# Linear attention ahead of a gated convolution: channels on partitions, four heads on quarters of the array, norms by way of DRAM

## The chip, the cores and the metric

The kernel runs on one core of a Trainium2 chip. The metric is the device time of one execution in microseconds (us), taken as the median of several runs. A profile is one execution recorded by the hardware profiler; its span reaches from the first to the last instruction. TensorE is called PE (its weight loads PEld), VectorE DVE, ScalarE ACT, GpSimd POOL, SyncE SP.

## What is computed

Three blocks follow one another on 8 batches of 576 tokens. The first is linear attention with 8 heads of 64 channels and a root-mean-square norm on each head; the second is a causal convolution gate over 512 channels; the third mixes along the tokens.

```
kv  = einsum('bhsd,bhse->bhde', k, v)
out = einsum('bhsd,bhde->bhse', q, kv)
x   = out / sqrt(mean(out * out, -1) + 1e-6) * g_norm      # heads side by side: 512 channels
gate = sigmoid(sum_k conv_w[k] * x shifted by 4-k tokens)
x   = (gate * (x @ w_val)) @ w_out
theta = x @ w_theta
y   = w_tok_r @ (x * cos(theta)) + w_tok_i @ (x * sin(theta))
u   = x + y;  result = u + max(u @ w_ch, 0)
```

The arrays come in float32, the weights in float64 words that the kernel decodes to float32 itself. Large products are made in three passes of float32r (high times high, low times high, high times low); the attention's own products are float32, which the trace shows as two records per product.

## The kernel before

The work has two stages. Stage one goes over the batches i = 0 to 7 and makes, for each, attention, value product, gate and output product; its result goes to DRAM (ydram). Stage two reads it back and does the token mixing (theta, u, c). The change lies in stage one alone.

In stage one the four weight chunks of w_val (wv) and of w_out (wo) are fetched, decoded on DVE (L92 to L96) and split into high and low parts (L67, L68). In one pass of the loop (L346) these steps follow one another on PE:

- attention(i+1), L173: for each of five chunks of 128 tokens (the last has 64) four products q times bd, where bd holds the kv of two heads on the diagonal of a 128x128 block. The result o has tokens on partitions and 512 channels along the row. ACT or DVE takes the squares and sums them per head (L184, L185, L189), twelve small DVE instructions make 1/sqrt by an integer start and three Newton steps (L197 to L203), and DVE multiplies o by it into xn (L207).
- value(i), L246: twelve products for each of four blocks m of 128 output channels and each half h of 288 tokens (v, L242 to L244), gated on DVE (g, L255) and split (gh, gl). The gate of block m comes from conv (L229): one ACT instruction, four DVE instructions (acc, L233), a sigmoid on ACT. Two convs are made ahead, the other two within value.
- key_value, L157: k times v for pairs of heads of later batches (kvp, L166), on two halves of the array's columns, three or four pairs in a pass.
- transposes(i+1), L214: xn is transposed on PE (xt, L222), which brings channels onto partitions; ACT writes xh and x, DVE the low part xl (L226). Then come two convs.
- first(i), L261: the output product (y), moved by ACT (yo, L267) and stored by SP.

PSUM is one pool of eight banks, given out in turn. A scheduler places each engine's instructions; waits on one engine's list are in order, and SP issues nearly all transfers in one list. The decoding of the weights of stage two (tk, wt) is put in at low priority in passes 1 to 5.

Of the kernel before, what the change touches and what calls it, by code (L numbers as in the profile page):

```python
# [11 lines left out]
I32 = mybir.dt.int32  # L12
# [12 lines left out]
CH = [(c * P, min(P, S - c * P)) for c in range(5)]  # L25
# [17 lines left out]
SUMS_ON_VECTOR = (range(5), (2, 4), ())  # L43
# [5 lines left out]
def attention_moe_holo_kernel(ctx, tc, kvm, kvt, qt, gn, w_val, conv_w, w_out, w_th, w_tok, w_ch, outT):  # L49
# [20 lines left out]
    def fetch(pool, src, width, name, tag=""):  # L70
# [31 lines left out]
    def weight_chunk(pool, tiles, src, k, name, scale=None, raw=None):  # L102
# [4 lines left out]
        if scale is None:  # L107
# [5 lines left out]
    ident = con.tile([P, P], F32, tag="ident", name="ident")  # L113
    make_identity(nc, ident)
# [11 lines left out]
    stdram = [dr.tile([P, DM], F32, tag=f"st{b}", name=f"st{b}") for b in range(0, B, 2)]  # L126
    tokdram = dr.tile([P, 9 * S], F32, tag="td", name="td")
# [5 lines left out]
    bds = []  # L133
    for i in range(NBD):
        t = pa.tile([P, NP, P], F32, tag=f"bd{i}", name=f"bd{i}")
        nc.gpsimd.memset(t, 0.0)
        bds.append(t)
# [19 lines left out]
    def key_value(b, kv, p0=0):  # L157

        ps = bank(f"kvp{b}_{p0}")
# [8 lines left out]
        bd = bds[b % NBD]  # L168
        psv = ps[:, 0:n * D].rearrange("p (a e) -> p a e", a=n)
        nc.scalar.activation(bd[0:D, p0:p0 + n, 0:D], psv[0:D], AF.Copy)  # L170
        nc.scalar.activation(bd[D:P, p0:p0 + n, D:P], psv[D:P], AF.Copy)

    def attention(b, q):  # L173
        bd = bds[b % NBD]
        ss = px.tile([P, 5, 8], F32, tag="ss", bufs=2, name=f"ss{b}")
        nc.gpsimd.memset(ss[D:P, 4, :], 1.0)
        po = []
        for c, (s0, n) in enumerate(CH):
            o = bank(f"o{b}_{c}")
            for p in range(NP):  # L180
                nc.tensor.matmul(o[:n, p * P:(p + 1) * P], q[p][:, s0:s0 + n], bd[:, p, :], start=True, stop=True)  # L181
# [382 lines left out]
```

## Time and profile before

| what | value |
|---|---|
| three runs | 754.7 to 756.11 us, median 755.47 us |
| the profiled execution's own time | 757.18 us |
| its span | 755.4 us |
| PE busy | 726.1 us (96%) |
| DVE busy | 534.8 us (71%) |
| ACT busy | 391.7 us (52%) |
| DMA | 97.58 MB, mean 129 GB/s |

Busy time is the union of an engine's records, and records of PE overlap, since a product's end is modelled; so the steps from start to start are what PE really spends. A busy time divided by its count is the cost of one instruction in a dense run; the mean is the length of one record. Idle time of an engine is put down to what ended last ahead of it.

### The profile page before, as it was taken

To read this page: it belongs to the slowest core of one execution; us is meant where nothing else is said; L and a number is where in the kernel's file an instruction comes from. 1 tells how busy PE (TensorE), PEld (TensorE's weight loads), DVE (VectorE), ACT (ScalarE), POOL (GpSimd) and SP (SyncE) were. 2 spreads that over 40 slices of the span, in tenths; PEclk is the share of its full clock that TensorE was granted. 3 is DMA by queue.
4 is the path that set the end of the run, shared out by engine and by line. 5 is a ranking of instruction groups with operands and counts; after the bars stand their busy time and mean duration, and the time that the engine had idled before them with its cause. 6 is when DMAs were issued, how large, how long until landed. Compare 5 with 4: busy or idle time off the path is not lost.

```text
span 755.4 us, 14634 instructions
## 1 busy us (share of the span) xinstructions
PE 726.1 (96%) x5584; PEld 697.9 (92%) x5584; DVE 534.8 (71%) x1045; ACT 391.7 (52%) x1173; POOL 16.4 (2%) x64
## 2 busy tenths in 40 slices
PE   2798999999999999999999999999999999999998
PEld 1797899999999999979899899899999999998998
DVE  4698888989899989769883873853853934936504
ACT  2366779787787876466541650621732513614301
POOL 2001000000000000000000000000000000000000
PEclk9889999999999999999999999999999999999999
DMA  9868644655544126634327034063051161160101
GB/s 297 274 190 271 215 160 139 203 186 170 178 139 149 64 89 161 209 109 120 127 88 205 2 125 112 19 187 87 17 162 61 62 169 50 58 177 4 64 1 63
DMA packets 77542, 97.58 MB, mean 129 GB/s; under 512 B 11168, under 2 KB 50208, under 8 KB 77472
## 3 DMA queue, kind: packets, MB, share of 16 engines
q1 hardware_dynamic: 76896, 94.55, 40.9%
q0 software_dynamic: 576, 2.10, 0.9%
q8 instruction: 44, 0.72, 0.4%
q14 instruction: 26, 0.21, 0.1%
HBM read 65.66 MB, written 30.97 MB: 128 GB/s over the span
## 4 chain that ended last, share of the span: by engine, by line
PE 88%; DMA 4%; ACT 4%; DVE 3%; issue 0%; SPq 0%; POOL 0%; DVEq 0%; ACTq 0%; POOLq 0%
PE u L467 10%; PE u L466 10%; PE u L465 10%; PE c L244 4%; PE c L242 4%; PE c L243 4%; PE v L242 4%; PE y L242 4%; PE o L181 4%; PE v L243 4%; PE y L243 4%; PE v L244 4%; PE y L244 4%; PE th L413 3%; PE th L411 3%; PE th L412 3%
## 5 line engine op out<-in xcount | busy, mean ns | idle before, releaser
L470 DVE TENSOR_TENSOR f<-u,f 128x288 f32<-128x288 f32 x64 | 26.5, 454 | 131.8 <-PE u L467 131.7
L67 ACT ACTIVATE uh<-f 128x288 fp32r<-128x288 f32 x64 | 26.1, 443 | 155.7 <-DVE f L470 155.7
L233 DVE SCALAR_TENSOR_TENSOR acc<-x,cw,acc 128x576 f32<-128x576 f32 x128 | 95.6, 810 | 1.1 <-ACT acc L231 1.1
L242 PE MATMUL y<-gh,woh 128*128 128x288 f32 x256 | 76.9, 302 | 1.6 <-ACT woh L67 0.9
L242 PE MATMUL v<-xh,wvh 128*128 128x288 f32 x256 | 77.4, 302 | 0.0
L243 PE MATMUL v<-xh,wvl 128*128 128x288 f32 x256 | 76.4, 298 | 0.0
L243 PE MATMUL y<-gh,wol 128*128 128x288 f32 x256 | 76.3, 299 | 0.0
L244 PE MATMUL v<-xl,wvh 128*128 128x288 f32 x256 | 75.8, 296 | 0.0
L244 PE MATMUL y<-gl,woh 128*128 128x288 f32 x256 | 75.6, 297 | 0.0
L242 PE MATMUL c<-uh,wch 128*128 128x288 f32 x256 | 75.4, 295 | 0.0
L244 PE MATMUL c<-ul,wch 128*128 128x288 f32 x256 | 75.4, 295 | 0.0
L243 PE MATMUL c<-uh,wcl 128*128 128x288 f32 x256 | 75.4, 294 | 0.0
L189 ACT ACTIVATE junk<-o 128x64 f32<-128x64 f32 (+1 forms) x264 | 55.1, 250 | 4.2 <-PE o L181 3.5
L189 ACT ACTIVATION_READ_ACCUMULATOR junk<-o 128x1 f32 (+1 forms) x264 | 53.7, 232 | 0.0
L242 PEld LDWEIGHTS y<-gh,woh 128*128 128x128 f32 x256 | 48.5, 190 | 2.5 <-ACT woh L67 1.0
L413 PE MATMUL th<-wth,yl 128*128 128x512 f32 x128 | 50.2, 393 | 0.0
L411 PE MATMUL th<-wth,yh 128*128 128x512 f32 x128 | 50.1, 391 | 0.0
L412 PE MATMUL th<-wtl,yh 128*128 128x512 f32 x128 | 50.0, 391 | 0.0
L242 PEld LDWEIGHTS v<-xh,wvh 128*128 128x128 f32 x256 | 48.9, 191 | 1.2 <-ACT junk L189 1.0
L243 PEld LDWEIGHTS v<-xh,wvl 128*128 128x128 f32 x256 | 48.9, 191 | 0.0
L243 PEld LDWEIGHTS y<-gh,wol 128*128 128x128 f32 x256 | 48.8, 191 | 0.1
L244 PEld LDWEIGHTS v<-xl,wvh 128*128 128x128 f32 x256 | 48.8, 191 | 0.0
(189 smaller groups left out, 2115.2 us busy)
## 6 DMA issues: line engine op xcount, KB each, us to landing
kv<-in_kvm_dram SPq DMA_DIRECT2D x32, 512.0 KB, 6.5
q<-in_qt_dram SPq DMA_DIRECT2D x32, 288.0 KB, 4.8
yd<-yo SPq DMA_DIRECT2D x64, 144.0 KB, 2.3
f<-yd SPq DMA_DIRECT2D x32, 288.0 KB, 3.4
out_dram<-f SPq DMA_DIRECT2D x64, 144.0 KB, 1.8
sd<-fT SPq DMA_DIRECT2D x64, 128.0 KB, 2.5
yt<-sd SPq DMA_DIRECT2D x8, 1024.0 KB, 5.4
raw_tk<-in_w_tok_dram SPq DMA_DIRECT2D x10, 512.0 KB, 5.4
```

Of the source, the lines that this page charges most:

```text
L181: nc.tensor.matmul(o[:n, p * P:(p + 1) * P], q[p][:, s0:s0 + n], bd[:, p, :], start=True, stop=True)
L189: nc.scalar.activation(junk[:n], o[:n, h * D:(h + 1) * D], AF.Square, scale=0.125, accum_out=ss[:n, c, h:h + 1])
L233: nc.vector.scalar_tensor_tensor(a, x[:, m, k:k + S], cw[:, m * 5 + k:m * 5 + k + 1], a, ALU.mult, ALU.add)
L242: nc.tensor.matmul(ps[:, :HS], wh[:, m, ks], xh[:, k, tsl], start=(k == 0), stop=False)
L243: nc.tensor.matmul(ps[:, :HS], wl[:, m, ks], xh[:, k, tsl], start=False, stop=False)
L244: nc.tensor.matmul(ps[:, :HS], wh[:, m, ks], xl[:, k, tsl], start=False, stop=(k == 3))
L411: nc.tensor.matmul(ps, yh[:, k, :], wth[0][:, k, :], start=(k == 0), stop=False)
L412: nc.tensor.matmul(ps, yh[:, k, :], wth[1][:, k, :], start=False, stop=False)
L413: nc.tensor.matmul(ps, yl[:, k, :], wth[0][:, k, :], start=False, stop=(k == 3))
L465: nc.tensor.matmul(ps[:, :HS], zh[:, ms], wkh[:, j, sl], start=(i == 0), stop=False)
L466: nc.tensor.matmul(ps[:, :HS], zh[:, ms], wkl[:, j, sl], start=False, stop=False)
L467: nc.tensor.matmul(ps[:, :HS], zl[:, ms], wkh[:, j, sl], start=False, stop=(i == 8))
```

## The change

- q times kv is turned round: kv of a head pair (kvs, 64x64 each) is the stationary operand and q moves in halves of 288 tokens, so that o has channels on partitions. Four heads use the four quarters of the array: the rows by the head's place in its pair, the columns by the pair (tile_position). A block o_h_g takes a pair of PSUM banks, for half h of the tokens and half g of the channels.
- The transposes (xt) and the identity are gone. ACT writes squares (sq) and, times g_norm, x itself from o.
- The sums of squares are made on PE: 64 products per batch with an indicator (ind) of 32 columns, each over 36 tokens, on quarters of the array's columns (ss, L219).
- The twelve DVE instructions stay, on 128x36. Their result y goes to DRAM (rd) and comes back spread over the 64 channels of each head (yb, 1.18 MB in two transfers). DVE then multiplies x by yb (L247), ACT and DVE split it (xh, xl).
- Channels now lie in another order: head pairs are mixed in blocks of 128. So the rows and columns of wv, wo and the conv weights are fetched in that order (mixed=True), in four transfers per chunk, half issued by SP and half by ACT.
- PSUM of stage one is three pairs of banks (o, v, y in turn) and two single banks (kvp, sums). v, g, gh, gl, yo are made for 576 tokens at once instead of twice 288. The kv buffers go from five to four.
- attention(i+1) is a generator: value(i) runs one block of it ahead of each m.

The names in the rows below carry the buffer number at the end; o_0_1 is half 0, channel half 1. On PE, in pass 2, this is where y of batch 2 ends and v begins, after the change:

```order
L266 MATMUL y_3_1940<-gl_1553,woh 128x288
L206 MATMUL o_0_0_2030<-q_0_1532,kvs_1359 64x288 x2
L206 MATMUL o_0_0_2030<-q_1_1534,kvs_1359 64x288 x2
L264 MATMUL v_0_2038<-xh_1834,wvh 128x288
L265 MATMUL v_0_2038<-xh_1834,wvl 128x288
L206 MATMUL o_0_1_2073<-q_2_1536,kvs_1359 64x288
L266 MATMUL v_0_2038<-xl_1835,wvh 128x288
```

Before, the twenty products of o stood in one run between y and v; now they lie in pieces between the products of v, two of which stand ahead of the first that needs xl.

On DVE, ahead of the last batch, before the change (y_3663 is 1/sqrt, acc the conv, fT belongs to stage two; the g and gl are the last of batch 6):

```order
L207 TENSOR_TENSOR xn_4_3686<-o_4_3649,y_3663 64x512
L68 TENSOR_TENSOR gl_3689<-g_2_3770,gh_3688 128x288
L255 TENSOR_TENSOR g_3_3803<-v_3_0_3804,acc_3_3763 128x288
L255 TENSOR_TENSOR g_3_3803<-v_3_1_3820,acc_3_3763 128x288
L226 TENSOR_TENSOR xl_3839<-x_3836,xh_3838 128x4x128
L68 TENSOR_TENSOR gl_3689<-g_3_3803,gh_3688 128x288 x2
L226 TENSOR_TENSOR xl_3839<-x_3836,xh_3838 128x4x128 x3
L226 TENSOR_TENSOR xl_3839<-x_3836,xh_3838 128x4x64
L275 STREAM_TRANSPOSE fT_0_4031<-f_4026 128x1024
L233 SCALAR_TENSOR_TENSOR acc_0_3880<-x_3836,cw,acc_0_3880 128x576
```

and after it:

```order
L69 TENSOR_TENSOR gl_3376<-acc_3_3459,gh_3375 128x576
L231 TENSOR_TENSOR t_3576<-t_3576,hm_3577 128x36
L232 SCALAR_TENSOR_TENSOR y_3575<-t_3576,y_3575 128x36
L247 TENSOR_TENSOR x_3377<-x_3377,yb_3591 128x2x576 x2
L69 TENSOR_TENSOR xl_3623<-x_3377,xh_3622 128x1152
L255 SCALAR_TENSOR_TENSOR acc_0_3630<-x_3377,cw,acc_0_3630 128x576
L69 TENSOR_TENSOR xl_3623<-x_3377,xh_3622 128x1152
```

The multiplication by 1/sqrt (xn before, x<-x,yb now) stood ahead of the last g and gl of batch 6; now it comes behind them, and the trip by DRAM lies between 1/sqrt and it, with no other instruction for DVE in between.

On SP, the trip itself in pass 5, after the change:

```order
L234 DMA rd_96<-y_3151 128x36
L421 DMA td<-dst_tk_2462 128x512
L291 DMA yd_75<-yo_0_3288 128x576
L93 DMA raw_tk_2925<-in_w_tok_dram 128x1024
L238 DMA yb_3167<-rd_96 64x4x576 x2
L291 DMA yd_75<-yo_1_3316 128x576
```

None of rd and yb was there before; yb stands behind the first store of y and a weight load.

The core of the diff:

```diff
+    ind = pa.tile([P, 16, 32], F32, tag="ind", name="ind")
+    nc.gpsimd.memset(ind, 0.0)
+    for i in range(2):
+        for t in range(16):
+            nc.gpsimd.memset(ind[i * D:(i + 1) * D, t, 16 * i + t:16 * i + t + 1], 1.0)
...
-            t = px.tile([P, 2, 5, P], F32, tag="kv", bufs=5, name=f"kv{b}_{p}")
+            t = px.tile([P, 2, 5, P], F32, tag="kv", bufs=4, name=f"kv{b}_{p}")
...
+        for h in range(2):
+            sl = slice(h * HS, (h + 1) * HS)
+            for g in range(2):
+                o = two_banks(f"o{b}_{h}_{g}")
+                for i in range(2):
+                    for j in range(2):
+                        rows = slice(j * D, (j + 1) * D)
+                        mm = nc.tensor.matmul(o[i * D:(i + 1) * D, j, :], kv[rows, 2 * g + i, :], q[2 * g + i][rows, sl],
+                                              start=True, stop=True, tile_position=(j * D, i * D))
+                ch = slice(2 * g, 2 * g + 2)
+                sq[h, g] = px.tile([P, 2, HS], F32, tag="sq", bufs=4, name=f"sq{b}_{h}_{g}")
+                nc.scalar.activation(sq[h, g], o, AF.Square, scale=0.125)
+                nc.scalar.activation(x[:, ch, PAD + h * HS:PAD + (h + 1) * HS], o, AF.Copy, scale=gsb)
+                if (h, g) != (1, 1):
+                    yield x
+
+        with tc.issue_after(mm.ins):
+            for t in range(16):
+                for k in range(NM):
+                    ts = slice(t % 8 * TB, (t % 8 + 1) * TB)
+                    nc.tensor.matmul(sums[32 * k:32 * (k + 1), :], ind[:, t, :], sq[t // 8, k // 2][:, k % 2, ts],
+                                     start=(t == 0), stop=(t == 15), tile_position=(0, 32 * k))
...
+        nc.sync.dma_start(out=rdram[b], in_=y)
+        yb = px.tile([P, NM, S], F32, tag="yb", bufs=1, name=f"yb{b}")
+        for i in range(2):
+            src = rdram[b].rearrange("(k i s) x -> i k (s x)", i=2, s=16)[i]
+            nc.sync.dma_start(out=yb[i * D:(i + 1) * D], in_=src.unsqueeze(0).to_broadcast([D, NM, S]))
+        yield x, yb
+
+    def normalize(b, x, yb):
...
+        for g in range(2):
+            ch = slice(2 * g, 2 * g + 2)
+            v = x[:, ch, PAD:]
+            last = nc.vector.tensor_tensor(v, v, yb[:, ch, :], ALU.mult)
+            parts(xh[:, ch, :], xl[:, ch, :], v)
+        return (x, xh, xl), last
...
         for m in range(NM):
+            between()
+            g = sg[m]
+            ps = two_banks(f"v{b}_{m}")
             for h in range(2):
+                product(ps[:, h], wv, m, xh, xl, h * HS)
+            halves = lambda t: t.rearrange("p (h s) -> p h s", h=2)
+            nc.vector.tensor_tensor(halves(g), ps, halves(g), ALU.mult)
+            parts(gh[:, m, :], gl[:, m, :], g)
```

More of the change, by code (lines that the diff above doesn't have):

```diff
@@ L24 @@
 PAD = 4
-CH = [(c * P, min(P, S - c * P)) for c in range(5)]
+TB = 36
 EPS = 1e-6
@@ L126, in attention_moe_holo_kernel @@
     stdram = [dr.tile([P, DM], F32, tag=f"st{b}", name=f"st{b}") for b in range(0, B, 2)]
+    rdram = [dr.tile([P, TB], F32, tag=f"rd{b}", name=f"rd{b}") for b in range(B)]
     tokdram = dr.tile([P, 9 * S], F32, tag="td", name="td")
@@ L157, in key_value @@
     def key_value(b, kv, p0=0):
-        ps = bank(f"kvp{b}_{p0}")
+        ps = pk.tile([P, 512], F32, tag="pk", name=f"kvp{b}_{p0}")
         n = len(kv)
@@ L167, in key_value @@
                                      start=(c == 0), stop=(c == 4), tile_position=(0, j * D))
[L168 to L171, printed above, removed]
+        if b not in kvs_of:
+            kvs_of[b] = pa.tile([P, NP, D], F32, tag="kvs", bufs=NBD, name=f"kvs{b}")
+        nc.scalar.activation(kvs_of[b][:, p0:p0 + n, :], ps[:, 0:n * D].rearrange("p (a e) -> p a e", a=n), AF.Copy)
@@ new lines, in attention @@
+        x = pa.tile([P, NM, PAD + S], F32, tag="x", bufs=2, name=f"x{b}")
+        nc.gpsimd.memset(x[:, :, 0:PAD], 0.0)
+        sums = pk.tile([P, 512], F32, tag="pk", name=f"ss{b}")[:, :TB]
+        sq = {}
+        for h in range(2):
[3 more added lines that the diff above has]
+                for i in range(2):
+                    for j in range(2):
+                        rows = slice(j * D, (j + 1) * D)
[7 more added lines that the diff above has]
+                    yield x
@@ L200, in attention @@
+        t = px.tile([P, TB], F32, tag="t", bufs=2, name=f"t{b}")
+        hm = px.tile([P, TB], F32, tag="hm", bufs=2, name=f"hm{b}")
+        nc.vector.tensor_scalar(ss, sums, EPS, None, ALU.add)
+        nc.vector.tensor_scalar(y.bitcast(I32), ss.bitcast(I32), -0.5, RSQRT_BITS, ALU.mult, ALU.add)
+        nc.vector.tensor_scalar(hm, ss, -0.5, None, ALU.mult)
         for _ in range(3):
@@ L365, in attention_moe_holo_kernel @@
             kvs[b, p] = load_kv(b, (p,))[0]
-        if i + 1 < B:
-            xn, last = attention(i + 1, qs.pop(i + 1))
-        if i > 0:
-            gs = value(i, *xs, sg)
+        nxt = attention(i + 1, qs.pop(i + 1)) if i + 1 < B else iter(())
+        if i == 0:
+            gs = value(i, *xs, sg, lambda: None)
+            for k in range(WOFIRST):
+                weight_chunk(px, wo, w_out, k, "wo", raw=raw[f"o{k}"])
+            xyb = list(nxt)[-1]
+        else:
+            got = []
+            gs = value(i, *xs, sg, lambda: got.append(next(nxt, None)))
+            xyb = got[-1]
         if i == 0:
```

136 lines of the change are left out of this document (46 added, 90 removed).

## The prediction

> **What bounds the kernel now.** I read the page's busy times first, then the windows of stage one batch by batch (cut where o of the next batch begins), then PE's timeline, and last DVE's groups and its timeline ahead of the last batch.
>
> ```profile
> span 755.4 us, 14634 instructions
> PE 726.1 (96%) x5584; PEld 697.9 (92%) x5584; DVE 534.8 (71%) x1045; ACT 391.7 (52%) x1173; POOL 16.4 (2%) x64
> ```
>
> ```profile
> core 0: us, PE busy (x) PEld busy (x) DVE busy (x) ACT busy (x) POOL busy (x), PEclk, DMA share, GB/s
> 122.35:156.99 34.64, 34.64 (x314) 33.88 (x313) 32.34 (x68) 28.43 (x124) 1.14 (x5) 1.00 0.57 182
> 156.99:191.94 34.95, 34.93 (x314) 33.85 (x313) 32.09 (x68) 28.32 (x122) 1.14 (x5) 1.00 0.55 179
> 262.12:294.73 32.61, 32.61 (x255) 32.08 (x253) 28.35 (x60) 27.03 (x120) 0.12 (x1) 1.00 0.36 108
> 294.73:320.20 25.47, 25.47 (x195) 25.47 (x193) 21.48 (x41) 9.69 (x23) 1.20 (x2) 1.00 0.69 202
> ```
>
> PE never pauses from 122 to 320 us: five batches take (294.73 - 122.35) / 5 = 34.5 us each. But DVE is busy 32 of these 34.6 us. So stage one is PE's, with DVE 7% behind: a batch in which DVE has to stand and wait for a few us becomes DVE's. The head of the program is another matter:
>
> ```profile
> 0.00:20.00 20.00, 5.07 (x80) 4.51 (x80) 9.30 (x15) 5.42 (x8) 5.42 (x23) 1.00 0.92 301
> 20.00:30.00 10.00, 8.82 (x106) 8.38 (x102) 4.14 (x13) 3.96 (x8) 0.61 (x2) 1.00 0.90 267
> 30.00:40.00 10.00, 7.05 (x46) 6.49 (x47) 9.28 (x24) 4.95 (x10) 0.99 (x4) 0.61 0.58 212
> 60.00:87.00 27.00, 22.85 (x257) 20.84 (x252) 22.75 (x50) 18.66 (x52) 2.65 (x10) 0.94 0.79 247
> ```
>
> There DMA is 0.8 to 0.9 busy and PE idles. Stage two, from 320 us on, is untouched; I give it no change.
>
> **The change part by part.**
>
> *PE's work in a batch.* Rows of PE's timeline:
>
> ```profile
> 86.94 4.75 PE L181 MATMUL o<-bd,q 128*128 128x128 f32 x40
> 104.60 1.97 PE L166 MATMUL kvp<-kv 128*64 128x64 f32 x60
> 106.67 2.90 PE L222 MATMUL xt<-ident,xn 128*128 128x128 f32 x20
> 139.62 0.29 PE L243 MATMUL v<-xh,wvl 128*128 128x288 f32 x1
> 139.75 0.29 PE L244 MATMUL v<-xl,wvh 128*128 128x288 f32 x1
> 279.65 2.30 PE L222 MATMUL xt<-ident,xn 128*128 128x128 f32 x20
> ```
>
> ```profile
> 139.97 0.39 PE L166 MATMUL kvp<-kv 128*64 128x64 f32 x6
> ```
>
> Gone: o 4.7 and xt 2.3 to 2.9, together 7.3 us. Added: 16 products q by kvs, two records each. A record of 128 columns steps by (4.75 - 0.27) / 39 = 0.115 us, 0.9 ns a column, so one of 288 columns costs some 0.25 us. How far do quarters run together? The nearest row is kvp, whose halves alternate two records by two: 60 records of 64 columns step by (1.97 - 0.22) / 59 = 0.030 us, where 0.9 ns a column would be 0.057. So two run at a time. That can be because the array holds just two tiles in that row, or because products start in order and a second record waits for the first of its tile, which then holds back those behind it. I take the second for four quarters: a run of n products costs (n + 1) x 0.25. Three whole blocks (1.25 each) and o_0_1, which the order cuts into 1, 1 and 2 (1.75), make 5.5 us. Each change of tile shape costs 0.22 - 0.13 = 0.09 us (last v at 139.75, kvp at 139.97, against a step of 0.13); six pieces among v are twelve changes, 1.1 us. The 64 sums have two records of 36 columns: between 0.033 (two at a time at 0.9 ns a column) and kvp's 0.060 us a product, I take 0.045, 2.9 us. New: 9.5 us, net +2.2. PE's own period goes from 34.5 to 36.7 us.
>
> The bounds of the quarters: all four at a time, 0.5 us a block (3.0 us with the split block) and sums at 1.1, PE's period is 34.5 - 7.3 + 3.0 + 1.1 + 1.1 = 32.4; one at a time, 16 x 0.5 = 8.0 and 3.8, it is 40.1. The Trainium skill (TensorE: Matmul & The Clock Gate, Part 3: Packing small matmuls) says that products on different row and column groups start some 4 ns apart and all run concurrently; by that rule the 16 products would cost about 2 us. It is weighed as a rival below; kvp's row shows two together and cannot show four.
>
> *The chain by DRAM.* Groups of DVE and transfers that price it:
>
> ```profile
> L233 DVE SCALAR_TENSOR_TENSOR acc<-x,cw,acc 128x576 f32<-128x576 f32 x128 | 95.6, 810 | 1.1 <-ACT acc L231 1.1
> L255 DVE TENSOR_TENSOR g<-v,acc 128x288 f32<-128x288 f32 x64 | 28.6, 451 | 7.1 <-PE v L244 5.3 <-ACT acc L234 1.1 <-ACT junk L189 0.7
> L226 DVE TENSOR_TENSOR xl<-x,xh 128x512 fp32r<-128x512 f32 x32 | 21.8, 682 | 3.2 <-ACT x L225 2.8
> L202 DVE TENSOR_TENSOR t<-t,hm 128x40 f32<-128x40 f32 x24 | 4.8, 198 | 0.2
> L189 ACT ACTIVATE junk<-o 128x64 f32<-128x64 f32 x216 | 45.4, 257 | 4.2 <-PE o L181 3.5
> ```
>
> ```profile
> kv<-in_kvm_dram SPq DMA_DIRECT2D x32, 512.0 KB, 6.5
> yd<-yo SPq DMA_DIRECT2D x64, 144.0 KB, 2.3
> yt<-sd SPq DMA_DIRECT2D x8, 1024.0 KB, 5.4
> td<-dst_tk SPq DMA_DIRECT2D x1, 32.0 KB, 1.4
> ```
>
> From 0.45 at 288 and 0.68 at 512 elements a step of 576 is 0.75 and one of 1152 some 1.34 us. Count from T = 0, the end of the sums. v_3 takes 24 x 0.134 = 3.2 us, and its g and gl stand among the twelve small instructions (0.2 each), so 1/sqrt is done at 6 us, at 8 where decoding stands between them. The way out is like td, 1.6 us with the issue; the way back is 1.18 MB, by yt 6.4 us, behind up to one load of 0.5 MB (2 us). So yb lands at L = 14 to 17, I take 15.5. PE meanwhile does v_3, kvp (2) and y (12.9) and is at the next o_0_0 at 18. From L on DVE sets the pace: two multiplications (2.7) and xl (1.3) to L + 4.0; then nine conv steps (6.7) and the second xl, and g of v_0 ends at L + 12.8. Only then is its pair of banks free for o_1_0, three pairs being given out in turn. o_1_0 (1.4), v_2 (3.2), o_1_1 (1.3) and the sums (3.1) follow, and the next T is L + 21.9 = 37.4 us. Both limits are near each other, 36.7 and 37.4; I take 37.5 for the period, +3.0 x 5 = **+15 us**, with ends of +5 (35.5) and +25 (39.5).
>
> *Ahead of the last batch.* DVE's timeline:
>
> ```profile
> 281.59 0.69 DVE L226 TENSOR_TENSOR xl<-x,xh 128x512 fp32r<-128x512 f32 x1
> 286.80 1.24 DVE L275 STREAM_TRANSPOSE fT<-f 128x1024 f32<-128x1024 f32 x1
> 310.07 1.05 DVE L68 TENSOR_TENSOR gl<-g,gh 128x288 fp32r<-128x288 f32 x2
> ```
>
> From xl of batch 7, just as y of batch 6 begins, DVE works 29.5 us with hardly a pause to the last gl, and y of batch 7 starts at 307.5 only because xl began so early. After the change y(6) begins at T + 3.4, and xl only at L + 2.7 = T + 16.4 (L is 13.7, no load ahead): 13 us later. Fewer, wider instructions give back 1.2. **+12 us**, 9 to 14.
>
> *The head.* Rows of PE's timeline and of the waits:
>
> ```profile
> 21.20 6.70 PE L181 MATMUL o<-bd,q 128*128 128x128 f32 x39 [0.93 <-ACT bd L171]
> 32.95 4.29 PE L222 MATMUL xt<-ident,xn 128*128 128x128 f32 x20 [3.20 <-DVE xn L207]
> 37.17 1.33 PE L166 MATMUL kvp<-kv 128*64 128x64 f32 x20
> PE kvp L166 <- DMA kv<-in_kvm_dram: 15.7, 5, 7.1
> ```
>
> v(0) starts at 38.4. After: o(0) and its sums end near 30 us, 1/sqrt at 33; rd is issued behind the first loads (DMA 0.9 busy to 35) and lands at 36.5, yb goes behind a kv load and lands at 44.5, v(0) starts at 48.5. Its second half needs weight chunk 3, whose decoding is put behind the multiplication (issue_after) and ends at 44.5 + 18.6 = 63; v(0) ends at 69.5, o(1) with sums at 78. rd of batch 1 stands in SP's list behind three kv loads of batch 4, and these wait for buffers that the kvp of batch 3 frees (84): yb lands near 97, and y(1) ends 40 us later (21.9 + 18.1) at 137, where it ended at 122.35: **+15 us**. If neither hold-up bites, yb lands at 85.5: +3; with the loads slower, +22. Fetching the weights in smaller pieces and half by ACT is in that range.
>
> *What costs nothing.* ACT drops the 80 records of junk (L189) a batch, but was busy 28 of 34.6 us with nobody waiting: no gain. The kv buffers, indicator and memsets of POOL are early or idle work; if not, they are inside the head's range.
>
> **Sum:** +15 + 15 + 12 = +42 us on the span of 755.4. The profiled execution's own time was 757.18, the median 755.47, as good as the span; so 755.5 + 42 = 797.5, I say 798.
>
> **The rivals.**
>
> *Quarters four at a time.* PE's period 32.4; the chain is then 3.3 shorter after L (two blocks and the sums), 18.6 + 15.5 = 34.1, so -0.4 x 5 = -2. Head 13, last batch 12: +23, 778 us. For it: two halves do run together. Against: a product is two records, and they start in order. The rule of the Trainium skill quoted above gives this case.
>
> *The quarters don't run together* (the change doesn't do what it says): 40.1 us of PE a batch, +5.6 x 5 = 28, with 15 and 12 +55: 810. For it: nothing in the trace shows row halves together.
>
> *Faster: a short trip with full quarters.* The place is DVE's wait for yb. If yb lands by T + 9, which asks for less than 3 us for both transfers, the chain is 27.6 and PE alone sets 32.4: -2.1 x 5 = -10.5. xl(7) then starts 8.3 us after y(6) begins: +7. The head gains 5, because all kv of batch 0 are now loaded ahead of most weights: 755.5 - 8.5 = 747. It decides below about T + 10. Against it: 1 MB takes 5.4 us.
>
> **How the numbers follow.** My forecast 0.60, four at a time 0.16, no overlap 0.14, the short trip 0.10 (0.08 faster, 0.02 in its milder form within 0.2%, about what a measurement of this kernel can tell from no change). Slower is 0.90. My forecast's own ends are 755.5 + 3 + 5 + 9 = 772 and + 22 + 25 + 14 = 816, met together rarely; with 778 and 810 inside, and a little for what I priced least well (the head), the range is 768 to 822.
>
> **What would show it.** Right: DVE idle before L247 for some 6 to 8 us where no decoding fills it; PE waiting at v for xl and at o_1_0 for g; y(1) ending near 137, y(6) 187 us later, y(7) 37 us after y(6). Wrong: yb landing within 4 us of 1/sqrt; o_1_1 taking 0.6 us or 2.1 us instead of 1.3; v(0) starting at 42.

## The result: slower by 13.5%, and the profile after

| | before | after |
| --- | --- | --- |
| median, us | 755.21 (754.7 to 756.11, four runs) | 857.64 (855.13 to 859.85, four runs) |
| ratio | | 1.1354, 95% interval 1.1314 to 1.1394 |
| span of the profiled execution, us | 755.4 | 854.2 |

The forecast was 798 us, in a range of 768 to 822. The sign was right, and the size was more than twice the one forecast: 102 us where 42 were expected. The first lines of the page after, and the whole span cut at the ends of y of batches 1, 6 and 7:

```profile
span 854.2 us, 15488 instructions
...
PE 751.3 (88%) x6384; PEld 688.9 (81%) x6384; DVE 522.4 (61%) x926; ACT 339.3 (40%) x563; POOL 14.7 (2%) x83
```

```profile
core 0: us, PE busy (x) PEld busy (x) DVE busy (x) ACT busy (x) POOL busy (x), PEclk, DMA share, GB/s
0.00:161.05 161.05, 100.63 (x1245) 84.40 (x1245) 75.64 (x137) 52.95 (x83) 9.25 (x66) 0.84 0.68 184
161.05:379.81 218.76, 189.50 (x2021) 162.80 (x2020) 154.61 (x264) 101.51 (x155) 3.23 (x13) 0.88 0.47 139
379.81:419.98 40.17, 30.91 (x194) 29.70 (x193) 34.15 (x46) 17.69 (x27) 1.19 (x2) 0.87 0.69 207
419.98:854.20 434.22, 430.27 (x2930) 411.96 (x2928) 257.98 (x479) 167.11 (x299) 1.05 (x2) 1.00 0.31 89
```

Before, these stretches were 122.35, 172.4, 25.5 and 435.2 us. So y(1) ends 38.7 us later (forecast +15), the five batches that follow take 46.4 us more (forecast +15), the last batch 14.7 more (forecast +12), and stage two 1.0 less (forecast none). PE, which before never paused from 122 us to the end of stage one, is now idle for 29 of the 219 us and has only 0.88 of its clock there. What it waits for stands in its waits:

```profile
PE v L264 <- ACT xh L68: 54.9, 8, 14.7
PE kvp L185 <- DMA kv<-in_kvm_dram: 20.4, 6, 9.6
PE o L206 <- ACT x L211: 7.2, 2, 4.0
```

Eight times, once in each batch, the first product of v stands still for xh, the part of x that is made right after the multiplication by 1/sqrt. The first wait, 14.7 us, is the head's. One steady batch, followed back, is the same trip each time. From the chain of waits that ends with that multiplication in the fourth pass (batch 4; its sums ended at 230.5):

```profile
238.93 0.68 DVE dst_wt L106
239.61 0.12 DVE y L232
239.74 4.30 DMA rd<-y
244.06 0.60 SPq L238
244.65 0.04 issue
244.70 8.26 DMA yb<-rd
```

1/sqrt is ready 9.2 us after the sums, since its twelve small instructions alternate with the conv, g and the decoding of weights (dst_wt is a neighbour in the chain; in the head, with nothing between them, they take 2.5 us). The way out takes 4.3 us, and the way back 8.9 (244.06 to 252.96). SyncE's list shows what stands ahead of rd:

```profile
236.08 0.56 SPq L163 DMA_DIRECT2D kv<-in_kvm_dram  x1
236.98 0.54 SPq L164 DMA_DIRECT2D kv<-in_kvt_dram  x1
237.63 0.55 SPq L163 DMA_DIRECT2D kv<-in_kvm_dram  x1
239.74 0.33 SPq L234 DMA_DIRECT2D rd<-y  x1
...
244.06 1.26 SPq L238 DMA_DIRECT2D yb<-rd  x2
```

The loads of the next kv have just been issued. VectorE meanwhile runs out of work (its line for the multiplication: start, duration, and in brackets the idle time before it), and PE's line tells the rest:

```profile
253.05 2.63 DVE L247 TENSOR_TENSOR x<-x,yb 128x1152 f32<-128x1152 f32 x2 [9.22 <-DMA yb<-rd]
```

```profile
228.28 0.71 PE L206 MATMUL o<-q,kvs 64*64 64x288 f32 x8
228.93 1.61 PE L219 MATMUL ss<-sq,ind 128*32 128x36 f32 x128
230.47 0.40 PE L264 MATMUL v<-xh,wvh 128*128 128x288 f32 x1
...
248.65 0.71 PE L206 MATMUL o<-q,kvs 64*64 64x288 f32 x8
255.66 0.61 PE L264 MATMUL v<-xh,wvh 128*128 128x288 f32 x1 [6.30 <-ACT xh L68]
256.07 0.44 PE L265 MATMUL v<-xh,wvl 128*128 128x288 f32 x1
256.44 1.22 PE L206 MATMUL o<-q,kvs 64*64 64x288 f32 x2
...
258.00 0.44 PE L264 MATMUL v<-xh,wvh 128*128 128x288 f32 x1
258.24 0.44 PE L265 MATMUL v<-xh,wvl 128*128 128x288 f32 x1
```

Two things are to be seen. The new products are cheap: the eight records of a block o go by in 0.65 us (228.28 to 228.93), the 128 of the sums in 1.54. And behind the wait of 6.3 us every step is longer: the records of v follow each other every 0.24 us (258.00 to 258.24), where they came every 0.13 before it. (The 1.15 us of the two records of o is not the clock alone: they are one product, with no other quarter at work beside it.) The windows of this batch, cut at the wait and at the end of the slow steps, show the granted clock (the number after the five engines):

```profile
248.65:255.66 7.01, 0.71 (x9) 0.21 (x8) 2.61 (x3) 3.15 (x5) 0.00 (x0) 0.92 1.03 326
255.66:264.62 8.96, 8.96 (x29) 6.40 (x29) 8.96 (x12) 3.67 (x5) 0.00 (x0) 0.50 0.39 130
264.62:293.07 28.45, 28.39 (x377) 26.20 (x377) 19.09 (x40) 13.74 (x22) 1.04 (x4) 1.00 0.53 148
```

Behind this wait PE works 9 us at half its clock; in all five passes the 9 us behind the wait show a clock of 0.50 to 0.53. The Trainium skill (TensorE: Matmul & The Clock Gate, Part 1: The HAM clock gate) says that the clock falls to half after at least one idle window of some 3.4 us and comes back after at least one busy window of that length; the fall agrees with this row, and the way back took 9 us here.

### The profile page after: what moved, and what is told of

Its sections match the earlier page's. It is cut to its first block, busy times and chain, and to the rows that moved or that the text cites. A ratio compares the mean times of both kernels' runs of the same rounds, so it can differ in the third digit from the quotient of the medians.

```text
span 854.2 us, 15488 instructions
## 1 busy us (share of the span) xinstructions
PE 751.3 (88%) x6384; PEld 688.9 (81%) x6384; DVE 522.4 (61%) x926; ACT 339.3 (40%) x563; POOL 14.7 (2%) x83
## 3 DMA queue, kind: packets, MB, share of 16 engines
q1 hardware_dynamic: 79088, 102.03, 41.2%
## 4 chain that ended last, share of the span: by engine, by line
PE 65%; DMA 16%; DVE 10%; ACT 5%; issue 2%; SPq 1%; ACTq 0%; POOL 0%; DVEq 0%; POOLq 0%
PE u L494 9%; PE u L492 9%; PE u L493 9%; DMA yb<-rd 6%; PE c L266 4%; PE c L265 4%; PE c L264 4%; DMA rd<-y 4%; PE v L264 3%; PE v L266 3%; DVE acc L255 3%; PE th L440 3%; PE th L438 3%; PE th L439 3%; PE v L265 3%; PE o L206 3%
## 5 line engine op out<-in xcount | busy, mean ns | idle before, releaser
L264 PE MATMUL v<-xh,wvh 128*128 128x288 f32 x256 | 89.3, 350 | 63.7 <-ACT xh L68 54.9
L264 PEld LDWEIGHTS v<-xh,wvh 128*128 128x128 f32 x256 | 58.0, 227 | 73.6 <-ACT xh L68 58.4
L255 DVE SCALAR_TENSOR_TENSOR acc<-x,cw,acc 128x576 f32<-128x576 f32 x128 | 98.7, 810 | 0.0
L266 PE MATMUL v<-xl,wvh 128*128 128x288 f32 x256 | 87.4, 342 | 0.5 <-DVE xl L69 0.4
L265 PE MATMUL v<-xh,wvl 128*128 128x288 f32 x256 | 85.5, 334 | 0.0
L247 DVE TENSOR_TENSOR x<-x,yb 128x1152 f32<-128x1152 f32 x16 | 21.0, 1354 | 91.0 <-DMA yb<-rd 91.0
L266 PEld LDWEIGHTS v<-xl,wvh 128*128 128x128 f32 x256 | 57.1, 223 | 11.5 <-DVE xl L69 6.3
L265 PEld LDWEIGHTS v<-xh,wvl 128*128 128x128 f32 x256 | 58.0, 227 | 0.9 <-DVE acc L255 0.9
L206 PE MATMUL o<-q,kvs 64*64 64x288 f32 x256 | 42.6, 497 | 9.9 <-ACT x L211 7.2
```

What stands on the lines that cost most here:

```text
L206: mm = nc.tensor.matmul(o[i * D:(i + 1) * D, j, :], kv[rows, 2 * g + i, :], q[2 * g + i][rows, sl], start=True, stop=True, tile_position=( ...
L255: nc.vector.scalar_tensor_tensor(a, x[:, m, k:k + S], cw[:, m * 5 + k:m * 5 + k + 1], a, ALU.mult, ALU.add)
L264: nc.tensor.matmul(ps, wh[:, m, ks], xh[:, k, tsl], start=(k == 0), stop=False)
L265: nc.tensor.matmul(ps, wl[:, m, ks], xh[:, k, tsl], start=False, stop=False)
L266: nc.tensor.matmul(ps, wh[:, m, ks], xl[:, k, tsl], start=False, stop=(k == 3))
```

## The experiments

My theory (A): the trip by DRAM is the loss. Its length L, from the end of the sums to yb's landing, sets the period, since whatever PE does beside it is shorter; in the head it comes on top of everything. The rival (B): the work on the chip is the loss, that is the quarter products, VectorE's chain or the half clock. Times are medians beside runs of the kernel before on the same chip (756 to 757 us); the stretches are those of the windows above, read from each run's profile. The kernels build on each other as told: e1 to e6 are edits of the changed kernel alone, e7 joins e3 and e5, e8 goes on from e1, e10 from e7, and e11 to e13 each build on the one before.

| run | median, us | ratio to before | y(1) ends | y(1) to y(6) | y(6) to y(7) | stage two |
| --- | --- | --- | --- | --- | --- | --- |
| before | 755.21 | 1 | 122.35 | 172.4 | 25.5 | 435.2 |
| after | 857.64 | 1.135 | 161.05 | 218.8 | 40.2 | 434.2 |
| e1_no_way_back | 766.82 | 1.013 | 129.54 | 170.4 | 26.0 | 436.6 |
| e2_pool_queue | 870.60 | 1.151 | 161.76 | 226.5 | 44.6 | 434.4 |
| e3_attention_first | 808.44 | 1.066 | 159.07 | 173.7 | 26.9 | 448.1 |
| e4_keep_warm | 842.24 | 1.114 | 163.12 | 201.8 | 41.2 | 437.9 |
| e5_head | 843.52 | 1.115 | 147.16 | 216.8 | 40.7 | 434.3 |
| e6_loads_behind | 843.10 | 1.116 | 158.45 | 204.0 | 38.8 | 437.0 |
| e7_all | 786.43 | 1.040 | 136.43 | 172.1 | 26.7 | 447.1 |
| e8_no_multiply | 760.03 | 1.006 | 127.69 | 166.8 | 26.8 | 436.6 |
| e10_early_q | 778.56 | 1.029 | 132.29 | 176.3 | 32.1 | 434.7 |
| e11_between_y | 767.71 | 1.014 | 137.72 | 165.4 | 25.5 | 434.6 |
| e12_trip_first | 783.18 | 1.037 | 143.76 | 174.1 | 25.5 | 434.6 |
| e13_q_free | 767.31 | 1.016 | 139.26 | 161.2 | 25.7 | 438.3 |

From e11 on the attention of batch 3 lies ahead of the end of y(1). So in e11 to e13 the stretch from y(1) to y(6) holds four attentions and not five (1862 records of PE where most others have some 2022), and some 4 us of PE, four blocks of 0.65 and the sums of 1.54, stand in the column before it.

**The way back left out (e1).** The two transfers of yb go, and x is multiplied by a constant tile of ones, so that the output lacks the norm; the rest stays.

```diff
         nc.sync.dma_start(out=rdram[b], in_=y)
-        yb = px.tile([P, NM, S], F32, tag="yb", bufs=1, name=f"yb{b}")
-        for i in range(2):
-            src = rdram[b].rearrange("(k i s) x -> i k (s x)", i=2, s=16)[i]
-            nc.sync.dma_start(out=yb[i * D:(i + 1) * D], in_=src.unsqueeze(0).to_broadcast([D, NM, S]))
-        yield x, yb
+        yield x, ones
```

> What is computed changes: the two transfers that bring 1/sqrt back are left out, and x is multiplied by a constant tile of ones, so that the output lacks the norm; the norm sums, 1/sqrt and its way to DRAM are still made. Theory A (the trip sets the period: from the end of the sums to yb's landing 22.5 us in the pass looked at, 8.9 of them for yb itself, and PE's own work in a batch is shorter): x no longer waits for anything after its copy, the PE's idle time ahead of the first v product (54.9 us in eight waits) goes, and the half clock after it; six y runs in the middle come 33 to 35 us apart where they came 43 to 45, y(1) ends near 135 to 145 where it ended at 161, and the whole takes 755 to 785 us. Rival B (the quarter products, the small VectorE operations and the order on ACT cost the time, not the trip): the periods stay over 41 us and the whole over 835.

766.82 us: of the 102 us that the change cost, 91 (857.64 - 766.82) are gone. The windows of the five batches in the middle, and of one of them:

```profile
129.54:299.98 170.44, 163.83 (x2023) 148.60 (x2023) 152.05 (x261) 99.41 (x154) 3.11 (x12) 0.99 0.44 144
...
```

```profile
199.06:233.57 34.51, 32.70 (x414) 29.62 (x413) 33.38 (x59) 20.89 (x33) 1.04 (x4) 1.00 0.60 192
```

The five periods average 34.1 us, the clock is whole, and nobody waits for xh. That settles A against B. In the head y(1) still ends 7.2 us later than before the change, so 31.5 of the 38.7 us there go with the way back. But the run is still 1.3% (1.0% to 1.6%) over the kernel before: a trip of which only the way out is left would not have paid either. Both PE (32.7) and VectorE (33.4) are busy nearly all of this batch, and that raised the question of what bounds it then.

**The multiplication left out too (e8).**

```diff
-            last = nc.vector.tensor_tensor(v, v, yb[:, ch, :], ALU.mult)
-            parts(xh[:, ch, :], xl[:, ch, :], v)
+            last, _ = parts(xh[:, ch, :], xl[:, ch, :], v)
```

> As the run without the way back, and the multiplication of x by the constant is left out too (two of 1.354 us on VectorE in each batch), so that the output lacks the norm altogether. Theory V (VectorE, busy 33.1 of 33.8 us in a pass, is what bounds the kernel once the trip is gone): a period falls by 2.5 to 3 us to about 31.5, 745 to 754 us, and below the kernel before by a per cent. Rival P (PE, whose busy time reads 32.7 us in the same pass, is the bound): the periods stay over 33.5 and the whole at 762 to 768.

760.03 us, the periods 33.4 on average: 0.7 us less a batch where theory V said 2.5 to 3. It lies between the two, much nearer to P. PE's line in one of its batches (195.22 to 229.04) shows why:

```profile
195.22 0.72 PE L208 MATMUL o<-q,kvs 64*64 64x288 f32 x8
...
207.91 1.60 PE L221 MATMUL ss<-sq,ind 128*32 128x36 f32 x128
...
216.66 0.40 PE L261 MATMUL y<-gh,woh 128*128 128x288 f32 x1 [0.48 <-ACT gh L68]
...
217.85 0.41 PE L263 MATMUL y<-gl,woh 128*128 128x288 f32 x1 [0.40 <-DVE gl L69]
```

o, v, sums and kvp follow each other without a pause, but y begins 1.9 us after the last v, with only kvp between, and waits inside for g of the last m: it takes 14.3 us where it took 12.8 before the change. Before the change the transposes (2.6 us) lay in that gap; that they covered it is my reading of the two traces, and no run tests it. By this count the change takes 7.3 us of o and xt from PE, adds 2.6 of o, 1.5 of sums and some 0.5 of shape changes (an estimate, from 0.09 each), and gives back 1.4 at y: 1.3 us less a batch, where the periods show 1.1. VectorE alone is not the bound.

**Another queue (e2).** rd and yb are issued by GpSimd.

```diff
-        nc.sync.dma_start(out=rdram[b], in_=y)
+        nc.gpsimd.dma_start(out=rdram[b], in_=y)
...
-            nc.sync.dma_start(out=yb[i * D:(i + 1) * D], in_=src.unsqueeze(0).to_broadcast([D, NM, S]))
+            nc.gpsimd.dma_start(out=yb[i * D:(i + 1) * D], in_=src.unsqueeze(0).to_broadcast([D, NM, S]))
```

> 1/sqrt goes out and comes back by GpSimd's queue and no longer stands behind the loads of kv, q and x on SyncE's. Theory A1 (the place behind the loads is what made the trip long: rd landed 4.3 us after its issue behind three loads of kv, yb 8.9 after its own; in the head rd was issued 7 us late behind the loads of q(1)): rd lands after about 2 us, yb after 6 to 7, 4 to 5 us less in each of five periods and 5 to 8 in the head, 825 to 835 us. Rival A2 (what makes the trip long is the bytes: 1.18 MB of yb and the loads share the same 16 DMA engines, whichever queue issues them): rd and yb take the same 13 us, only the head gains, 848 to 857 us.

870.60 us, 13 more than after: worse than both theories. The transfers' median times from issue to landing, and GpSimd's line in the same pass:

```profile
yb<-rd POOLq DMA_DIRECT2D x16, 576.0 KB, 9.8
...
rd<-y POOLq DMA_DIRECT2D x8, 18.0 KB, 4.8
```

```profile
240.38 0.56 POOL L234 DMA_DIRECT2D rd<-y  x1 [3.73 <-DVE y L232]
246.22 1.23 POOL L238 DMA_DIRECT2D yb<-rd  x2 [5.29 <-DMA rd<-y]
```

rd goes out as soon as y is there and still takes over 5 us for 18 KB. The head shows the same: rd(0) leaves at 40.9, 2.8 us earlier than after the change, and yb lands at 61.3 where it landed at 56.5. So it isn't the place in SyncE's list that makes it slow; A1 falls, and the bytes of A2 are nearer, with a surcharge that A2 had not. The Trainium skill (DMA: Bandwidth & Descriptors, Issuing engines are not separate DMA queues) says that transfers from all engines run on the same 16 DMA engines and interleave there; this row agrees. Why yb is slower yet, 9.8 against 7.4 in the changed kernel, no run tells apart.

**The loads behind the trip (e6).**

```diff
+            with tc.issue_after(trip[0].ins):
+                for b, p in more:
+                    kvs[b, p] = load_kv(b, (p,))[0]
```

(trip[0] is the second transfer of yb; the same loads ahead of value(i) are gone.)

> From the second pass on, the loads of kv for the next batches are issued behind the two transfers of yb; before, the scheduler put them ahead of rd. Theory A1 (it is the loads in front, on the DMA engines and not on a queue, that make rd take 4.3 us and yb 8.9): rd lands 1.5 to 2 us after its issue, as in the order with the attention first, yb after 6 to 7; L falls from 22.5 to 16 to 18 us, the period from 44.4 to 38 to 40, the whole to 825 to 840 us. Rival A2 (the loads are only sent back, and the kv products, which then wait for them, hold up y): the wait of kvp for kv grows from 20 us to over 40 and the whole stays at 850 to 862.

843.10 us, 14.5 less than after, 3 us above the range that A1 gave; kvp waits for kv 20.9 us where it waited 20.4 after the change, so A2 falls. In the second pass (sums of batch 2 end at 140.3) the chain reads:

```profile
146.22 1.52 DMA rd<-y
147.76 0.58 SPq L238
148.40 7.53 DMA yb<-rd
```

L is 155.9 - 140.3 = 15.7 us, and this batch's period is 37.7 (158.45 to 196.11). The forecast had L = 15.5 and a period of L + 21.9 = 37.4: where the trip has the forecast length, the forecast period comes out. In the other four passes L is 19 to 22: rd is short there too (yb follows it after 1.9 to 2.4 us), but 1/sqrt is ready only 8.4 to 9.9 us after the sums, and the way back takes 8.4 to 11.2. So the loads in front explain the length of rd; they do not explain that of yb.

**Keeping PE busy in the wait (e4).**

```diff
+        if i + 1 < B:
+            warm = pk.tile([P, 512], F32, tag="pk", name=f"warm{i}")
+            for n in range(48):
+                nc.tensor.matmul(warm[:, :HS], wv[0][:, 0, 0:P], wv[0][:, 1, 0:HS], start=True, stop=True)
```

> 48 products of 128x128 by 128x288 that nobody reads follow each y, about 6.4 us at 0.134 each, so that the PE is busy where it waited 5 to 7 us for x. Theory A with the clock as a part of the price (granted clock 0.50 in the 9 us after the wait, v records every 0.24 us in place of 0.134): the first v products run at the full step, 2 to 4.5 us less in each period, 835 to 848 us. Rival (the half clock is beside the path, since the trip alone sets the period): no change, 855 to 860; or the dummies outlast the wait and delay v by a microsecond or two each, up to 870.

842.24 us, 15.4 less. PE's line in the pass of batch 4:

```profile
243.36 6.48 PE L413 MATMUL warm<-wvh 128*128 128x288 f32 x48
249.77 0.71 PE L206 MATMUL o<-q,kvs 64*64 64x288 f32 x8
251.17 0.40 PE L264 MATMUL v<-xh,wvh 128*128 128x288 f32 x1 [0.68 <-ACT xh L68]
```

The granted clock in the 9 us from there on is 1.00, and the five batches take 16.9 us less, 3.4 each; 2 us go again in the head, 1 in the last batch and 4 in stage two (the profiled execution took 845.85 us). From yb's landing to the end of the next sums the five passes now take 18.8 to 19.1 us, where they took 21.6 to 22.4 after the change. So the half clock behind the wait costs some 3 us a batch, and it lies on the path.

**The attention first (e3).** All of attention(i+1) is issued ahead of value(i).

```diff
-            got = []
-            gs = value(i, *xs, sg, lambda: got.append(next(nxt, None)))
-            xyb = got[-1]
+            xyb = (list(nxt) or [None])[-1]
+            gs = value(i, *xs, sg, lambda: None)
```

> All of the next batch's attention, sums, 1/sqrt and trip are issued before the value products of this batch, so that value, kv products and y (about 28 us of PE) lie beside the trip. Theory A (the trip of 22.5 us alone sets the period): it is hidden, PE's wait at the first v product goes, and the period falls to PE's own work, 32 to 35 us; with the head as it is (y(1) near 155 to 165) the whole takes 795 to 820 us. Rival B (ACT and VectorE in series, the copy of o, the squares, the twelve small operations, the two parts, are the limit): the period stays over 41 us and the whole over 840.

808.44 us. The five batches take 173.7 us, 34.7 each, 1.3 more than before the change in all: with v, kvp and y beside it, the trip is hidden. What stays is the head (y(1) at 159.1) and a new wait at the start of stage two:

```profile
PE v L264 <- ACT xh L68: 15.8, 2, 14.3
PE u L491 <- ACT wkh L68: 12.1, 1, 12.1
```

The first is the head's, the second comes from the token weights, whose decoding has fallen behind.

**The head (e5).**

```diff
-START = "v0 k0 k1 v1 k2 k3 v2 q0 q1 q2 q3 v3 k4 c0 k5 k6 o0 k7 o1 o2 o3 q4 q5 q6 q7"
+START = "v0 k0 c0 k1 v1 k2 k3 v2 q0 q1 q2 q3 v3 k4 k5 k6 o0 k7 o1 o2 o3"
...
+    qs[1] = load_q(1)
     key_value(1, kvs.pop(1))
+    for n in range(WVFIRST, 4):
+        weight_chunk(px, wv, w_val, n, "wv", raw=raw[f"v{n}"], mixed=True)
     xs, last = normalize(0, *xyb)
     sg = [conv(0, m, xs[0]) for m in range(EARLY)]
-    with tc.issue_after(last.ins):
-        for n in range(WVFIRST, 4):
-            weight_chunk(px, wv, w_val, n, "wv", raw=raw[f"v{n}"], mixed=True)
```

> Only the head is rearranged: gsb and the conv weights are loaded third and not after k4, the loads of q(1) are issued behind rd(0) and no longer ahead of it, and the last chunk of w_val is decoded before x(0) is normalized and not after it. Theory A (of the 38.7 us that y(1) came late, most is the first trip with what is queued behind it: o(0) waited for gsb until 32 us, rd(0) stood 7 us behind the loads of q(1), the raw weight chunks were not freed until v(0) ran, and SyncE issued hardly any load from 57 to 71 us): v(0) starts at 46 to 52 us in place of 59, y(1) ends at 136 to 147 in place of 161, the periods stay at 43 to 45, and the whole takes 832 to 845 us. Rival B (the head is bound by the bytes that it loads, 200 to 250 GB/s in the first 80 us, so that what is put ahead only sends something else back): y(1) ends within 4 us of 161 and the whole takes 850 to 860.

843.52 us, y(1) at 147.2: 13.9 us earlier, nearly what A said, though v(0) starts at 56.3 only, since rd(0) now stands behind the chunks of w_out (issued at 41.8). The gain lies behind v(0): the sums of batch 1 end at 78.5 where they ended at 96.7. I put it down to what no longer waits behind the trip, the last chunk of w_val and the loads that its buffer held up; the three edits were not tried one by one.

**All of it together (e7)**, the attention first in the first pass too. The rank of the decoding, of which the expectation speaks, is unchanged in this kernel (LATER is still 1000).

```diff
         if i == 0:
+            xyb = list(nxt)[-1]
             gs = value(i, *xs, sg, lambda: None)
...
-            xyb = list(nxt)[-1]
```

> Attention first in every pass, the first one too, with the rearranged head and the decoding of the token weights at a higher rank (300 in place of 1000 behind). Theory A (the trip is all that the change lost, in the head as in the passes): PE works on o(1) and its sums while the first trip runs, y(1) ends at 135 to 145, the periods are 33 to 36, stage two starts without the 12.1 us wait for wkh that the run with attention first had, and the whole takes 765 to 782 us: no more than 1 to 3% over the kernel before. Rival B (with the trip hidden VectorE, busy 33 of 34 us in the run without the way back, or the loads, busy 65% of the DMA engines there, push every pass up): periods over 36.5 and the whole over 790.

786.43 us. y(1) ends at 136.4 and the five batches take 172.1 us, as before the change; the wait for wkh is still 10.5 us, and without it the time would lie in the range of A. o(1) waited for q until 49 us, for more of it until 57, and ran to 60.7.

**q(1) early and the rank of 300 (e10).** q(1) stands in the first list of loads again, and the load of it behind rd(0) goes.

```diff
-START = "v0 k0 c0 k1 v1 k2 k3 v2 q0 q1 q2 q3 v3 k4 k5 k6 o0 k7 o1 o2 o3"
+START = "v0 k0 c0 k1 v1 k2 k3 v2 q0 q1 q2 q3 v3 k4 k5 k6 k7 q4 q5 q6 q7 o0 o1 o2 o3"
...
-LATER = 1000
+LATER = 300
```

> As the run with all of it, with two edits. The token weights are decoded 300 ranks behind and not 1000 (the run before was meant to have this and had not); and in the head q(1) is loaded ahead of the raw chunks of w_out again, since o(1) waited there for q until 60.7 us. Theory A (what is left of the loss, 30 us, is 14 in the head, 10.5 in the wait for wkh at the start of stage two, and the rest spread): the wait for wkh goes under 2 us, o(1) is done before 48 us, v(0) starts at 48 to 54 in place of 63, y(1) ends at 122 to 130, and the whole takes 756 to 770 us. Rival B (the loads bind the head, and w_out, sent back, then holds up y(0)): y(1) stays at 133 to 138 and the whole at 772 to 780, the wait for wkh alone being gone.

778.56 us. The wait for wkh is gone and o(1) is done at 45.3, but v(0) starts at 63.5: rd(0) is issued at 44.2 and yb lands at 60.1. The five batches take 176.3 us now, 4 more, and the last one 32.1, 5 more; kvp waits for kv 31.5 us in all, 10 more than in the run before. The whole is B's, though y(1) is a little better than B said.

**o between the parts of y (e11).** Each block of attention(i+2) is issued ahead of one part of y(i), the sums ahead of the last.

```diff
-    def first(b, gh, gl, ms):
+    def first(b, gh, gl, ms, between=lambda: None):
         for m in ms:
+            between()
...
+        nxt, got = attention(i + 2, qs.pop(i + 2)) if i + 2 < B else iter(()), []
+        step = lambda: got.append(next(nxt, None))
...
-        first(i, *gs, range(n, NM))
+        first(i, *gs, range(n, NM), step)
+        xyb = got[-1]
```

> As the run with the early q, and from the third batch on the four blocks of o are not issued in a row but one ahead of each of the four parts of the y before (of batch i+2 in pass i), with the sums ahead of its last part, so that their copies on ACT lie beside products. Theory A (with the trip hidden, 1 to 3 us of a period are the four blocks in a row waiting for their copies, 3.8 to 5.4 us where they take 2.6 alone, and y waiting for g): the periods fall from 34 to 32 to 33, the whole 6 to 12 us below the run with the early q, 748 to 762, about the kernel before. Rival B (VectorE, 31.6 us busy in 34, or ACT, or the loads keep the period): periods stay at 34 and the time is that of the run with the early q within 3 us.

767.71 us, 10.9 less than the run with the early q: theory A's gain, from a time that was higher than A had counted on. What o waits for the copies of y on ACT falls from 10.1 us to 2.3, as A said. But the periods are not 32 to 33: the four from y(1) to y(5), with a whole attention in each, take 34.7 us on average, where they took 36.2 in the run with the early q and 34.9 before the change. The last batch takes 25.5, 6.6 less.

```profile
137.72:303.08 165.36, 156.42 (x1862) 144.53 (x1862) 147.67 (x253) 96.09 (x149) 3.11 (x12) 1.00 0.65 191
303.08:328.53 25.45, 25.45 (x193) 25.45 (x193) 18.85 (x30) 7.78 (x12) 1.19 (x2) 1.00 0.70 205
```

The stretch of 165.4 us is 7 us shorter than before the change and y(1) ends 15.4 us later, but some 4 us of each are the attention that moved: the passes gain 3 us and the head loses 11. All that is lost, 7.7 us of the profile's span, is in the head.

**The first trip first in line (e12).**

```diff
+    with tc.issue_after(trip[0].ins):
+        for n in range(1, 4):
+            raw[f"o{n}"] = fetch(px, w_out[:, n, :], DM, f"wo_{n}", mixed=True)
...
+    with tc.issue_after(trip[0].ins):
+        kvs[2] = load_kv(2)
...
-            qs[i + 2] = load_q(i + 2)
+            with tc.issue_after(trip[0].ins):
+                qs[i + 2] = load_q(i + 2)
```

> As the run with o between the parts of y, and in the head the chunks of w_out but the first, kv(2) and q(2) are issued behind the first trip; in the later passes q(i+2) is issued behind the trip before it. Theory A (from v(0) on, the run before took 264 us to the end of y(7) and the kernel before the change 282, so that the whole of what is still lost, 26 us, lies ahead of v(0): there 1/sqrt was made at 38.1 us, rd was issued at 45.9 behind loads, yb landed at 60): rd is issued by 40 us, yb lands by 51, v(0) starts at 51 to 55 in place of 64, and the whole takes 750 to 758 us, level with the kernel before or up to 1% under it. Rival B (the bytes of the head bind: w_out and kv(2), sent back, hold up y(0) and the kv products by as much): v(0) starts earlier but y(1) still ends at 134 to 140, and the whole takes 763 to 770.

783.18 us, slower. In the head it did what A said: rd at 37.95, yb landed at 51.3, v(0) at 54.0. But the last edit sent q back in every pass, and o waited for it 23.1 us in all.

**q free again (e13)**, the last edit above only for i = 0.

```diff
-            with tc.issue_after(trip[0].ins):
+            with tc.issue_after(trip[0].ins) if i == 0 else ExitStack():
```

> As the run with the first trip first in line, but only q(2) is issued behind the trip; the q of the later passes are free again (there, o waited 23.1 us for q in six waits, 11.0 in one, and y(1) came at 143.8 though y(0) had come 9 us earlier than in the run with o between the parts of y). Theory A (the sending back of q in the later passes cost all of that, and the head is what still parts the run with o between the parts of y from the kernel before): the wait of o for q falls under 5 us, the periods return to 34, y(1) ends at 127 to 132, and the whole takes 753 to 762 us, level with the kernel before. Rival B (the loads that the first trip sends back come due in the second pass whatever their order): the wait moves to kvp for kv, y(1) stays at 136 to 144, and the whole takes 765 to 783.

767.31 us. The wait for q is 2.3 us. The five batches from y(1) to y(6), and the first of them:

```profile
139.26:300.49 161.23, 155.97 (x1862) 144.44 (x1862) 151.40 (x259) 97.70 (x152) 3.51 (x13) 1.00 0.65 192
```

```profile
139.26:171.93 32.67, 32.24 (x414) 29.56 (x414) 32.55 (x56) 21.01 (x33) 1.32 (x4) 1.00 0.69 207
```

v(0) starts at 57.3, 6.9 us earlier than in the run with o between the parts of y, y(0) ends 5.2 us earlier, and yet y(1) ends 1.5 us later. The two numbers are B's, but its mechanism is not seen: from v(0) to the end of y(1) kvp waits 0.5 us for kv, and most of the other waits of PE there are for work of ACT and VectorE (2.5 us for the copies of o, 1.1 for g, 0.9 for kvs). What slows the second pass is open. The four passes to y(5) take 33.5 us on average, 1.4 less than before the change, and y(1) ends 16.9 us later, some 4 of them for the attention that moved. The whole stays 1.55% (1.29% to 1.81%) over the kernel before. No version here beats it.

## Why the prediction was wrong

**The trip, +15 forecast, +46 measured: the step that failed.** It said "1/sqrt is done at 6 us, at 8 where decoding stands between them", "the way out is like td, 1.6 us", "the way back is 1.18 MB, by yt 6.4 us, behind up to one load of 0.5 MB (2 us)", so L = 14 to 17, and took 15.5. (The upper ends of its terms add up to 18.) In the pass shown these were 9.2, 4.3 and 8.9, and L is 22.5. In the five passes they were 7.8 to 9.3, 2.4 to 5.1 and 8.7 to 9.7 us, and L was 21.0 to 23.2: together 33 us above five times 15.5, where the forecast missed by 31. The period was to be L + 21.9, and from yb's landing to the end of the next sums it took 21.6 to 22.4 us (in the pass shown 21.9, to 274.9). So the whole excess of a period is L. The run with the loads behind the trip shows the other side: L = 15.7 gives 37.7.

Each of the three terms was too small by about 2 us or more. 1/sqrt was slow because its small instructions alternate with more of VectorE's work than the forecast put between them. For rd the error was to price it by a row in which it travels with little beside it, though the kernel loads 2 to 3 kv tiles just there: it takes 1.5 us in the run with the attention first and 4.5 in the median after the change. For yb the runs show the length, and not the reason.

**The term behind L was right by two errors.** The products were forecast two at a time (1.3 us a block, 3.1 the sums); measured are 0.65 and 1.54, nearer to the 0.5 and 1.1 of four at a time, the rival that the forecast had given 0.16. What this saved behind L (two blocks and the sums, some 3 us) was eaten by the clock, which the forecast left at full: in the run that keeps PE busy the same stretch takes 18.8 to 19.1 us, and that rival's working gave 18.6. Nor did VectorE set the pace there, as forecast. o_1_0 was to wait for g of v_0 until 12.8 us behind yb's landing; in the pass shown it started 15.7 behind it (268.69), straight after the last product of v_1, since v_0 had run at half clock. That 21.9 came out is luck.

**The head, +15 forecast, +38.7 measured.** Forecast were rd landing at 36.5, yb at 44.5, v(0) at 48.5 and y(1) at 137. SyncE's list in the head:

```profile
39.70 3.99 SPq L172 DMA_DIRECT2D q<-in_qt_dram  x4
43.77 0.39 SPq L234 DMA_DIRECT2D rd<-y  x1
...
48.31 1.25 SPq L238 DMA_DIRECT2D yb<-rd  x2
```

The sums end at 36.3 and not near 30, because ACT's first copy of o(0) waited for gsb until 32.3, and rd then stands behind four loads of q(1) in order. rd lands at 48.3, yb at 56.5, and v(0) starts at 59.2, at half clock. The place in the list is not all of it, since on GpSimd's queue rd left earlier and yb landed later; the loads beside it (the DMA engines are 0.99 busy from 40 to 60 us) are the likelier cause, which no run shows by itself. What hung on v(0) moved with it: the sums of batch 1 end at 96.7 where 78 was forecast, and its yb lands at 121.8 where 97 was. From there to the end of y(1) it is 39 us, as forecast (40). The forecast had rd behind the first loads, but without those of q(1), and it did not have the wait for gsb. The head's edits gave back 13.9 us of it, and the attention first with them 10.7 more.

**The last batch, +12 forecast, +14.7 measured.** The mechanism held, and the size missed by L again: 13.7 us with no load ahead were forecast, and 17.4 measured, so that xl of batch 7 starts 16.9 us after y of batch 6 begins, where 13 were forecast. Stage two, none forecast, -1.0: right.

**The rivals.** Quarters four at a time: its products are nearly what happens, its 778 us isn't, since its trip was also 15.5 us. Quarters one at a time: out. The short trip, 747 us: out, and more than for its length. With no way back at all the kernel takes 766.8, and of the 2.1 us a batch that this rival gave PE the run shows 0.4 (periods of 34.1); I put the rest down to y, which waits for g where the transposes had been. In the order of the last run it was 1.4; its shortest full pass takes 32.7 us, with PE busy for 32.2 and VectorE for 32.6 of them, where the working with full quarters gave 32.4.

Of the signs named, VectorE was idle ahead of the multiplication for 9.2 us in the pass shown and 2.4 to 15.1 in the five, where 6 to 8 were named; y(6) came 219 us after y(1) (187), and y(7) 40.2 after y(6) (37). PE waited at v, for xh, but not at o_1_0 for g. A block takes 0.65 us: the sign that the quarters were wrong. v(0) and y(1) missed by 11 and 24 us.

**What stays open.** What bounds the head of the later versions is open: in the last two runs v(0) came earlier and y(1) did not, and no run loads less. Why the way back takes 8 to 11 us even with the loads behind it is open too.

## What to carry to other kernels

A step that goes to DRAM and comes back is a latency on a chain: price it by a row whose transfers have the same neighbours, and add the clock that PE loses while it waits. Issue the step a whole stage earlier, so that a stage of products lies beside it, before the order of anything else is tuned; here that took back 49 of 102 us with two lines. And look at what the removed work covered: the transposes that went had lain in the gap between v and y.

## What the runs showed of the hardware that was not expected

- Products of 64x64 by 64x288 in float32 on the four quarters: eight records in 0.65 us at full clock, 81 ns a record. A record of 288 columns by itself would take some 260 ns (an estimate, from the 0.9 ns a column of o before the change), so about three run at a time. The 128 records of the sums, 36 columns on quarters of the array's columns, take 12 ns each.
- 18 KB to DRAM and the semaphore back: 1.5 us in the median of the run with the attention first, where SyncE had issued no load for some 10 us; 4.5 after the change, behind loads of 0.5 MB; 4.8 on GpSimd's queue.
- Two reads of 576 KB that spread 18 KB over 64 partitions each: 6.4 to 7.6 us in the median on SyncE's queue, 9.8 on GpSimd's.
- A wait of 6.3 us cost PE half its clock for the next 9.0 us; 48 products that nobody reads kept it at 1.00.
